# Windowed attention with global keys, then a softmax-gated feed-forward layer: queries and keys in runs of six tokens, token order, sums of the first batch by TensorE, a new order

## The chip, the cores and the metric

The kernel runs on one core of a Trainium2 chip. The metric is device time in microseconds (us), lower is better. A core has TensorE (PE in the profile, its weight loads PEld), VectorE (DVE), ScalarE (ACT), GpSimd (POOL) and SyncE (SP); SP, ACT and POOL can issue DMA transfers, which share 16 DMA engines. Each engine works through its own instructions in program order.

## What is computed

Inputs are q, k and v for 4 batches, 8 heads, 768 tokens and 64 dimensions. Every token attends to the last 96 tokens and to the first 8 (the global ones), with a bias that falls with distance by a slope per head. The result, 3072 tokens of 512 features, goes through a layer of width 1024 that is gated by its own softmax and normalised.

```python
is_global = pos[None, :] < int(n_global)
is_local = (rel >= 0) & (rel < int(n_local))
keep = is_global | is_local
dist = np.where(is_global & ~is_local, float(n_local), np.abs(rel).astype(np.float32))
bias = -slopes[:, None, None] * dist[None, :, :]
scores = np.where(keep, scores + bias[None, :, :, :], -1000000000.0)
a = np.exp(scores - np.max(scores, axis=-1, keepdims=True))
a = a / (np.sum(a, axis=-1, keepdims=True) + 1e-09)
x = a @ v                                  # then as [3072, 512]
h = x @ w_in
e = np.exp(h - h_max)
solu = h * e / (np.sum(e, axis=-1, keepdims=True) + 1e-09)
ln = (solu - mu) / np.sqrt(var + 1e-06) * g_ln
out = ln @ w_out
```

## The kernel before

**An order made ahead of time.** The kernel function first describes its work as steps: an engine, an estimated duration, a priority, the steps it needs and the buffers it takes and gives back. `Plan.order` is a list scheduler: it plays the steps through in time by their estimates, at each moment starting on each free engine the ready step of the lowest priority number whose buffers are free, and the sequence that comes out is the program order of every engine, SP's DMA queue included. The priorities are the list `PRIO`, one number per step. On the chip an engine stops at the first instruction whose input isn't there, whatever the plan thought, and what stands behind it waits too. DMAs have a pool of 8 in flight.

**Attention.** Two heads make a pair, 4 pairs (`p`) per batch (`b`). Queries and keys are loaded in runs of 8 tokens on a partition (`load_heads`, L498; 96 partitions for 768 tokens), cast to f16 on POOL (L698), transposed on PE (L714, eight transposes of 96 columns), and copied out of PSUM on DVE: keys in token order (`kT`, L733, a strided copy), queries in the order [place in the run, run] (`qT`, L729, a copy in order). So everything that follows query columns is in that order too and is read through views such as `p (j g) -> p j g`: the bias window `bw`, the exponentials `eb`, the sums and the products. Only the last product (L1019) writes `xT` in token order. The first 256 tokens of batch 0 come by a different load (`load_first`, L504), token by token.

For each group of key blocks of 64 and each pair, PE adds the bias (L822) and the scores (L840), 64x64 matmuls on the four quarters of the array, and ACT takes the exponential to `eb` (L848). Batch 0 has three groups of 256 queries, the others two of 384. For each unit of queries (`ui`; the same widths):

- `gs`: scores of the global keys for all heads at once (L883), exponential to `eg` (L894);
- `sm`: sums of all heads on PE with matrices of ones (L905 local, L912 global), one row per head, then ln (L920) and exp(-x) (L923) on ACT, the reciprocals `rr`;
- the reciprocals go to DRAM (`store_recip`, L553) and come back with each head's row on 64 partitions (`spread_recip`, L559, two loads), the tile `rb`;
- `av` and `aw`: the products with the values (L992) and with the global values `vgz` (L979), in two halves for two pairs at a time, each pair in a PSUM bank of its own; a one-element copy on DVE (`tick`, L1002) lies between the halves. The global product is a matmul of 64 rows by 128 columns for each half;
- `nm_`: DVE multiplies each bank by `rb` into `xT` (L1019).

The values of a batch are loaded in pieces (`load_v`, L511) and cast (L783); the first and last 64 tokens of each odd head come for all four batches in two loads (`load_ends`, L518) and are cast per batch (L797).

**Feed-forward.** For each tile of 128 tokens: G1 on PE (L1051, eight matmuls of 512 columns), exp on ACT (L1058), the gate on DVE (L1061), the sum of squares on ACT (L1065), eight transposes on PE (L1072) and their copy to `uT` (L1076, four buffers), G2 (L1110), and the scaled eviction (L1116) and store (L1118). Before the first G2, `w_out` is scaled by `g` on DVE (L625, eight instructions), its mean is taken on PE (L631) and subtracted on DVE (L635).

Of the kernel before, what the change touches and what calls it, by code (L numbers as in the profile page):

```python
# [18 lines left out]
P = 128  # L19
BLK = 64  # L20
WIN = 160
JW = 8
BG = BLK // JW
WG = WIN // JW
# [89 lines left out]
"""  # L114


class Plan:
# [129 lines left out]
def kernel(  # L247
# [119 lines left out]
    def v3(ap):  # L367
        return ap.rearrange("p (j g) -> p j g", j=JW)
# [794 lines left out]
```

## Time and profile before

| | us |
|---|---|
| median of 3 runs | 222.46 |
| range | 219.66 to 223.21 |
| profiled execution, its time | 223.18 |
| profiled execution, its span | 221.5 |

| engine | busy us | share of the span |
|---|---|---|
| ScalarE | 112.9 | 51% |
| VectorE | 112.6 | 51% |
| GpSimd | 65.0 | 29% |

The span runs from the first to the last instruction that the profile holds. The page cuts it into 40 slices of 5.5 us; a digit is the busy share in tenths, and for the clock the share of TensorE's full speed that was granted. A timeline row has the start, the duration, the engine, the line, what is written and read, and the count of merged instructions; in brackets stands the idle time of the engine ahead of it and what ended it. A group's row has busy us and the mean duration in ns behind the bar, then idle time ahead of the group by what ended it.

### The profile page before, as it was taken

How to read it: one execution, taken by the hardware profiler on the slowest of the kernel's cores; microseconds unless marked ns; L12 is line 12 of the kernel's file. 1: busy time of each engine (PE TensorE's matmuls, PEld its weight loads, DVE VectorE, ACT ScalarE, POOL GpSimd, SP SyncE). 2: the span in 40 equal slices, each digit the busy share in tenths (PEclk: the TensorE clock that was granted, in tenths of full speed). 3: DMA queues.
4: the chain of work that ended last, by engine and by line, in shares of the span. 5: the costliest groups of instructions: out<-in, count | busy, mean ns of one | idle time of the engine just before them, and what ended most of it. 6: DMA issues, size and time to landing. Idle time of an engine off the chain costs nothing. (4 is left out here: it accounts for less than half of the span.)

```text
span 221.5 us, 6271 instructions
## 1 busy us (share of the span) xinstructions
PE 174.9 (79%) x2636; PEld 103.2 (47%) x2636; DVE 112.6 (51%) x238; ACT 112.9 (51%) x202; POOL 65.0 (29%) x140
## 2 busy tenths in 40 slices
PE   0036837677988979997879989779997999998890
PEld 0014416555664646564544546455555455434440
DVE  0465367223574554865534656352772368484540
ACT  2003302432682367693455888364785674566752
POOL 7854187430392166433072008300100000000000
PEclk9999995555999999999988999999999999999998
DMA  6999999994299992999995039631603156300222
GB/s 178 252 202 304 189 206 206 235 259 91 66 259 253 291 222 69 238 251 269 248 231 132 18 113 225 146 145 50 145 0 147 22 130 143 142 3 0 95 95 96
DMA packets 47387, 35.23 MB, mean 159 GB/s; under 512 B 32440, under 2 KB 37120, under 8 KB 47360
## 3 DMA queue, kind: packets, MB, share of 16 engines
q1 hardware_dynamic: 44560, 33.24, 61.1%
q0 software_dynamic: 544, 1.05, 2.9%
q10 hardware_dynamic: 2256, 0.56, 1.1%
q8 instruction: 20, 0.33, 0.7%
q14 instruction: 7, 0.06, 0.1%
HBM read 29.50 MB, written 6.39 MB: 162 GB/s over the span
## 5 line engine op out<-in xcount | busy, mean ns | idle before, releaser
L848 ACT ACTIVATE eb<-bank 128x960 f16<-128x960 f32 (+3 forms) x36 | 29.9, 856 | 48.2 <-PE bank L840 47.7
L1051 PE MATMUL bank<-w_in_sb,xT 128*128 128x512 f16 x192 | 47.1, 389 | 0.1
L1110 PE MATMUL bank<-gw_out_sb,uT 128*128 128x512 f16 x192 | 44.8, 379 | 1.0 <-DVE xT L1019 0.4
L1061 DVE SCALAR_TENSOR_TENSOR uu<-ef,bank 128x1024 f16<-128x1024 f16 x24 | 29.2, 1216 | 12.5 <-ACT ef L1058 12.4
L1058 ACT ACTIVATE ef<-bank 128x1024 f16<-128x1024 f32 x24 | 24.5, 1020 | 16.3 <-PE bank L1051 16.2
L1019 DVE TENSOR_TENSOR xT<-bank,rb 128x384 f16<-128x384 f32 (+1 forms) x36 | 25.2, 730 | 10.1 <-PE bank L992 5.0
L1110 PEld LDWEIGHTS <-uT 128*128 128x128 f16 x192 | 17.8, 97 | 21.3 <-DVE uT L1076 1.4
L1051 PEld LDWEIGHTS <-xT 128*128 128x128 f16 x192 | 17.9, 99 | 20.3 <-issue 1.9
L1065 ACT ACTIVATE sq<-uu 128x1024 f16<-128x1024 f16 x24 | 25.2, 1051 | 3.9 <-DVE uu L1061 3.7
L714 PE MATMUL bank<-ident,k 96*128 96x96 f16 (+2 forms) x136 | 10.2, 220 | 19.5 <-POOL k L694 10.9
L733 DVE COPY kT<-bank 128x768 f16<-128x768 f16 (+2 forms) x20 | 15.4, 769 | 19.4 <-PE bank L714 16.8
L992 PE MATMUL bank<-eb,v 64*64 64x160 f16 (+4 forms) x464 | 20.5, 230 | 4.1 <-DVE tick L1002 1.3
L1076 DVE COPY uT<-bank 128x1024 f16<-128x1024 f16 x24 | 16.4, 689 | 14.1 <-PE bank L1072 6.1
L698 POOL CAST k<-k 96x1024 f16<-96x1024 f32 (+1 forms) x16 | 16.5, 1035 | 23.1 <-PE bank L714 11.3
L698 POOL CAST q<-q 96x1024 f16<-96x1024 f32 (+1 forms) x16 | 16.4, 1036 | 19.9 <-PE bank L714 13.3
L1116 ACT ACTIVATE osb<-bank,rstd 128x512 f32<-128x512 f32 x24 | 15.9, 684 | 11.2 <-PE bank L1110 5.3
L714 PEld LDWEIGHTS <-k 96*128 96x128 f16 (+2 forms) x136 | 7.9, 106 | 23.6 <-POOL k L694 11.1
L992 PEld LDWEIGHTS <-v 64*64 64x64 f16 x464 | 11.8, 107 | 12.1 <-issue 8.1
L822 PE MATMUL bank<-bw,identb 64*64 64x160 f16 (+4 forms) x448 | 16.0, 251 | 0.8 <-DVE uu L1061 0.6
L783 POOL CAST v<-v 128x704 f16<-128x704 f32 (+2 forms) x24 | 13.4, 576 | 10.7 <-DMA v<-in_v_dram 10.0
L840 PE MATMUL bank<-qT,kT 64*64 64x160 f16 (+4 forms) x416 | 15.6, 250 | 0.5 <-DVE qT L729 0.5
L1072 PE MATMUL bank<-ident,uu 128*128 128x128 f16 x192 | 14.4, 219 | 1.8 <-DVE uT L1076 0.9
(82 smaller groups left out, 176.3 us busy)
## 6 DMA issues: line engine op xcount, KB each, us to landing
out_dram<-osb SPq DMA_DIRECT2D x24, 256.0 KB
q<-in_q_dram SPq DMA_DIRECT2D x12, 384.0 KB
k<-in_k_dram SPq DMA_DIRECT2D x12, 384.0 KB
rb<-rd SPq DMA_DIRECT2D x12, 384.0 KB
v<-in_v_dram SPq DMA_DIRECT2D x12, 192.0 KB
w_out<-in_moe_w_out_dram SPq DMA_DIRECT2D x4, 512.0 KB
v<-in_v_dram SPq DMA_DIRECT2D x12, 160.0 KB
rb<-rd SPq DMA_DIRECT2D x6, 256.0 KB
```

Source lines behind the costliest of these rows:

```text
L698: nc.gpsimd.tensor_copy(out=o[0:w], in_=a[0:w].rearrange("p h j d -> p j h d"))
L714: nc.tensor.transpose(out=pt[:, j * m : j * m + m], in_=src[0:m, j].rearrange("p h d -> p (h d)"), identity=ident[0:m, 0:m])
L822: nc.tensor.matmul(out=sc[o : o + 64, par, col : col + n * JW], lhsT=identb[r, r], rhs=v3(bw[r, p])[:, :, a : a + n], start=(par, h) not i ...
L848: ex["fn"] = (lambda ex=ex, qk=qk, gw=gw: nc.scalar.activation(out=eb[at(qk, "eb")][:, :, 0:gw], in_=big(qk)[:, :, 0:gw], func=AF.Exp, sca ...
L992: nc.tensor.matmul(out=o_[64 * h : 64 * h + 64, :, gl : gl + m], lhsT=vv[r, v_at(vi, h, c), d0 + d, :], rhs=view(eb[at(e_own[b, gi, d0 + d ...
L1019: nc.vector.tensor_tensor(out=xT[at(xt_own[b], "xT")][:, p, q0:q1].rearrange("p (g j) -> p g j", j=JW), in0=one(av, d)[:, 0:w].rearrange(" ...
L1051: nc.tensor.matmul(out=ph()[:, ts(fh, 512)], lhsT=xT[at(xt_own[b], "xT")][:, j, ts(t % NA, P)], rhs=w_in_sb[:, j, ts(fh, 512)], start=(j = ...
L1058: ex["fn"] = lambda g1=g1, t=t, ph=ph: nc.scalar.activation(out=ef[at(g1, "ef")], in_=ph(), func=AF.Exp, accum_out=s0[:, t : t + 1])
L1061: u["fn"] = lambda u=u, g1=g1, t=t, ph=ph: nc.vector.scalar_tensor_tensor(out=uu[at(u, "uu")], in0=ef[at(g1, "ef")], scalar=USC, in1=ph(), ...
L1065: sqs["fn"] = lambda u=u, t=t: nc.scalar.activation(out=sq, in_=uu[at(u, "uu")], func=AF.Square, accum_out=s2[:, t : t + 1])
L1076: el["fn"] = lambda lt=lt, el=el: nc.vector.tensor_copy(out=uT[at(el, "uT")].rearrange("p c f -> p (c f)"), in_=one(lt).bitcast(FP16))
L1110: nc.tensor.matmul(out=one(g2), lhsT=uT[at(el_x, "uT")][:, c, :], rhs=gw_out_sb[:, c, :], start=(c == 0), stop=(c == NFC - 1))
```

## The change

The parts of the change:

1. **Runs of six on 128 partitions.** Queries and keys are loaded in runs of 6 tokens (4 in the second part of batch 0), cast with 768 (512) instead of 1024 elements a partition, and transposed in 6 (4) pieces of 128 columns.
2. **Token order.** Queries are copied out of PSUM in token order like the keys. `bw`, `gmask`, `eb`, the sums and products are in token order, so the views with `j` and `g` go.
3. **Sums of batch 0 by TensorE** (`DIRECT`). In its three units there is no `sm`, no store and no spread. `av` and `aw` handle one pair at a time: one bank takes the products with the values, the other the same matmuls with a block of ones (`onesv`, `onesz`, two constants that POOL makes), so that each sum stands on all 64 partitions of its head. ACT takes ln and exp of that bank per pair, and DVE multiplies by it.
4. **Global products in quarters.** For each half the 64x128 matmul becomes two of 64x64 on different quarters of the array, in all batches.
5. `w_out` is scaled by `g` on ACT instead of DVE.
6. The loads of the end blocks are split by batch (eight instead of two); `uT` has seven buffers instead of four.
7. **A new order.** Estimates are changed, the plan may hold at most four bulk loads in flight (`ldq`, an estimate's limit, no wait on the chip), and all priorities are new.

```diff
-JW = 8
-BG = BLK // JW
-WG = WIN // JW
+RUN = 6
...
+LDQ = 4
...
-    uT = many(4, [P, NFC, P], FP16, "uT")
+    uT = many(7, [P, NFC, P], FP16, "uT")
...
+    def constants_direct():
+        nc.gpsimd.memset(onesv, 1.0)
+        nc.gpsimd.tensor_copy(
+            out=onesz, in_=bass.AP(tensor=pick.tensor, offset=pick.offset,
+                                   ap=[pick.ap[0], pick.ap[1], [0, D]]))
...
+    DIRECT = {(0, 0), (0, 1), (0, 2)}
...
     def view(ebt, rows, par, col, n, lo, m):
-        return ebt[rows, par, col : col + n * JW].rearrange("p (j g) -> p j g", j=JW)[
-            :, :, lo : lo + m]
+        return ebt[rows, par, col : col + n][:, lo : lo + m]
...
-    def load_heads(src, dst, b, p, lo, hi):
+    def load_heads(src, dst, b, p, lo, run):
         rows = src[b, 2 * p]
-        n = hi - lo
         nc.sync.dma_start(
-            out=dst[0:n].rearrange("g h j d -> g h (j d)"),
-            in_=bass.AP(tensor=rows.tensor, offset=rows.offset + lo * JW * D,
-                        ap=[[JW * D, n], [S * D, 2], [1, JW * D]]))
+            out=dst[:, 0 : 2 * run * D].rearrange("g (h x) -> g h x", h=2),
+            in_=bass.AP(tensor=rows.tensor, offset=rows.offset + lo * D,
+                        ap=[[run * D, P], [S * D, 2], [1, run * D]]))
...
-            wr.append(step("DVE", 484, 16000 + 100 * j, [w_out_st[j // 2], g_st] + bias_st + [far_st], lambda j=j:
-                           nc.vector.tensor_scalar(
-                               out=gw_out_sb[:, j, :], in0=w_out32[:, j, :],
-                               scalar1=g32[:, j : j + 1], scalar2=None, op0=ALU.mult)))
+            wr.append(step("ACT", 640, 16000 + 100 * j,
+                           [w_out_st[j // 2], g_st] + bias_st + [far_st], lambda j=j:
+                           nc.scalar.activation(
+                               out=gw_out_sb[:, j, :], in_=w_out32[:, j, :], func=AF.Copy,
+                               scale=g32[:, j : j + 1])))
...
+                    if natural:
+                        nc.vector.tensor_copy(out=d_, in_=pt)
+                    else:
+                        nc.vector.tensor_copy(
+                            out=d_.rearrange("p (g j) -> p g j", j=run),
+                            in_=pt.rearrange("p (j g) -> p g j", j=run))
...
+            direct = (b, ui) in DIRECT
+            sm, bi, bd = None, None, []
+            if not direct:
+                sm = step("PE", (cols + w) * 0.42 + 60, tS, deps + [ge, sums_st, sumg_st], None,
+                          take=("one", "lns"), mode="s")
...
+            for ti_, duo in enumerate([(p, None) for p in range(NPR)] if direct else
+                                      [(p, p + 1) for p in range(0, NPR, 2)]):
...
+                        pv = duo[d]
+                        pair = duo[0] if pv is None else pv
+                        o_ = one(av, d)[:, 0:w]
+                        for h in range(2):
+                            x = h ^ par
+                            r = slice(64 * x, 64 * x + 64)
+                            if i < 0:
+                                nc.tensor.matmul(
+                                    out=o_[64 * h : 64 * h + 64, x * n : x * n + n],
+                                    lhsT=(onesz[r, 2 * pair + h] if pv is None else
+                                          vgz[r, b, 2 * pair + h, :]),
+                                    rhs=eg[at(gs, "eg")][r, 0:hw_],
+                                    start=False, stop=False,
+                                    tile_position=(64 * x, 64 * h), skip_group_check=True)
+                                continue
...
+                                lhsT=onesv[r, :] if pv is None else vv[r, v_at(vi, h, c), pair, :],
...
+                if direct:
+                    ln = step("ACT", 110 + w, ta + 1000, [aw, table_st], None, take="lns",
+                              free=[(av, 1)])
...
+                    re = step("ACT", 140 + w, ta + 1500, [ln], None, take="rr",
+                              free=[(ln, "lns")])
...
+                    nm_ = step("DVE", 40 + 1.34 * w, ta + 600 + 100 * d,
+                               [aw] + ([re] if direct else bd), None,
...
+                        r_ = rr[at(re, "rr")][:, 0:w] if direct else rb[at(bi, "rb")][:, p, 0:w]
+                        nc.vector.tensor_tensor(
+                            out=xT[at(xt_own[b], "xT")][:, p, q0:q1], in0=one(av, d)[:, 0:w],
+                            in1=r_, op=ALU.mult)
```

More of the change, by code (lines that the diff above doesn't have):

```diff
@@ L666, in do_part @@
         def do_part(i, lo, hi, p):
[L667 to L669 removed]
+            natural = b == 0 and i == 0
+            run = (hi - lo) // P
+            n = hi - lo
             for nm, src, x32, x16, dst, dn in (("k", k, k32, k16, kT, "kT"),
@@ L677, in do_part @@
                             nc.sync if nm == "k" else nc.scalar, src, nat[nm], a, 2 * p, 4),
-                            512 * 22 / 16, -80000 + 100 * p, [],
-                            eng="SP" if nm == "k" else "ACT")[1] for a in range(2)]
+                            512 * 20 / 16, -80000 + 100 * p, [],
+                            eng="SP" if nm == "k" else "ACT")[1] for a in range(run)]
                     need = nat_dma[nm]
                 else:
-                    iss, dma = load(lambda s, src=src, x32=x32, nm=nm, p=p, lo=lo, hi=hi, b=b:
-                                    load_heads(src, x32[at(s, nm + "32_")], b, p, lo, hi),
-                                    2 * w * 110 / 16, t0 - 6000, [],
-                                    take=(nm + "32_",))
+                    iss, dma = load(lambda s, src=src, x32=x32, nm=nm, p=p, lo=lo, run=run, b=b:
+                                    load_heads(src, x32[at(s, nm + "32_")], b, p, lo, run),
+                                    256 * (12 + 10.5 * run) / 16, t0 - 6000, [],
+                                    take=(nm + "32_",), bulk=True)
@@ L759, in do_v @@
                     P * (hi - lo) * 21 / 16, t0 - 6000, [first] if first else [],
-                    take=() if first else ("v32_",))
+                    take=() if first else ("v32_",), bulk=True)
                 first = first or iss
@@ L918 @@
-            sm["fn"] = sums
-            ln = step("ACT", 110 + w, tS + 1000, [sm], None, free=[(sm, "one")])
-            ln["fn"] = lambda sm=sm, w=w: nc.scalar.activation(
-                out=lns[at(sm, "lns")][:, 0:w], in_=one(sm)[:, 0:w], func=AF.Ln)
-            re = step("ACT", 140 + w, tS + 1500, [ln], None, take="rr", free=[(sm, "lns")])
-            re["fn"] = lambda re=re, sm=sm, w=w: nc.scalar.activation(
-                out=rr[at(re, "rr")][:, 0:w], in_=lns[at(sm, "lns")][:, 0:w], func=AF.Exp, scale=-1.0)
@@ new lines, with sums @@
+            sm, bi, bd = None, None, []
+            if not direct:
+                sm = step("PE", (cols + w) * 0.42 + 60, tS, deps + [ge, sums_st, sumg_st], None,
+                          take=("one", "lns"), mode="s")
+                def sums(sm=sm, gs=gs, todo=todo, w=w, hw_=hw_, b=b):
+                    sp = one(sm)[:, 0:w]
+                    ng_ = hw_
+                    for i, (gi, c, par, col, n, lo, gl, m) in enumerate(todo):
+                        for p in range(NPR):
+                            nc.tensor.matmul(
+                                out=sp[32 * p : 32 * p + 32, gl : gl + m], lhsT=onesd[:, par, :],
+                                rhs=view(eb[at(e_own[b, gi, p], "eb")], slice(0, P), par, col, n, lo, m),
+                                start=(i == 0), stop=False,
+                                tile_position=(0, 32 * p), skip_group_check=True)
+                    for x in range(2):
+                        for p in range(NPR):
+                            nc.tensor.matmul(
+                                out=sp[32 * p : 32 * p + 32, x * ng_ : x * ng_ + ng_],
+                                lhsT=onesg[:, x, p, :],
+                                rhs=eg[at(gs, "eg")][:, 0:hw_],
+                                start=False, stop=(x == 1),
+                                tile_position=(0, 32 * p), skip_group_check=True)
+                sm["fn"] = sums
+                ln = step("ACT", 110 + w, tS + 1000, [sm], None, free=[(sm, "one")])
+                ln["fn"] = lambda sm=sm, w=w: nc.scalar.activation(
+                    out=lns[at(sm, "lns")][:, 0:w], in_=one(sm)[:, 0:w], func=AF.Ln)
+                re = step("ACT", 140 + w, tS + 1500, [ln], None, take="rr", free=[(sm, "lns")])
+                re["fn"] = lambda re=re, sm=sm, w=w: nc.scalar.activation(
+                    out=rr[at(re, "rr")][:, 0:w], in_=lns[at(sm, "lns")][:, 0:w], func=AF.Exp, scale=-1.0)
+                di, dd = load(lambda s, re=re, w=w: store_recip(rd[at(s, "rd")], rr[at(re, "rr")], w),
+                              60, tS + 2000, [re], take=("rd",), iss=600)
+                plan.release(re, "rr", [dd])
+                bi = None
+                for h in range(2):
+                    own_b = bi
+                    s_, d_ = load(lambda s, di=di, h=h, w=w, own_b=own_b: spread_recip(
+                        rb[at(own_b or s, "rb")], rd[at(di, "rd")], h, w),
+                        256 * (12 + 0.28 * w / 1.0) / 16, tS + 4000, [dd] + ([bi] if bi else []),
+                        take=() if bi else ("rb",), iss=600)
+                    bi = bi or s_
+                    bd.append(d_)
+                plan.release(di, "rd", bd)
@@ new lines @@
+            lastu = ui == len(UNITS[b]) - 1
+            if lastu:
+                plan.release(kg_own[b], "kg", kg_users)
+                for p in range(NPR):
+                    plan.release(own[p, "k"], "kT", qk_of[p])
+                    plan.release(own[p, "q"], "qT", qk_of[p])
+            turn_of = []
+            by = [[x for x in todo if x[2] == par] for par in range(2)]
+            turns = [[(i, d) for i in range(max(map(len, by))) for d in (0, 1)
+                      if i < len(by[ph ^ d])] for ph in range(2)]
```

320 lines of the change are left out of this document (127 added, 193 removed), and 170 rows, old and new, of the table PRIO.

## The prediction

> **What bounds the kernel now.** I read the page first (engines, slices), then the busy time by stage, then the timeline of batch 0's first unit from its last exponential to its first feed-forward matmul, then the groups by shape for prices.
>
> ```profile
> PE 174.9 (79%) x2636; PEld 103.2 (47%) x2636; DVE 112.6 (51%) x238; ACT 112.9 (51%) x202; POOL 65.0 (29%) x140
> ...
> PEclk9999995555999999999988999999999999999998
> DMA  6999999994299992999995039631603156300222
> ```
>
> TensorE (PE) has the most work, but the slices show two regimes: up to slice 9 (50 us) the DMA engines are full and PE's clock falls to half; after it the clock is whole. The same by stage (columns: length, then busy us and instructions of PE, PEld, DVE, ACT, POOL, clock, DMA share, GB/s):
>
> ```profile
> 9.90:35.00 25.10, 13.86 (x177) 8.11 (x178) 13.77 (x39) 3.66 (x7) 13.35 (x23) 0.95 1.11 223
> 35.00:56.70 21.70, 16.27 (x402) 12.30 (x402) 8.83 (x17) 8.35 (x14) 7.25 (x9) 0.51 0.87 185
> 56.70:100.00 43.30, 39.05 (x657) 24.45 (x649) 25.98 (x54) 27.59 (x51) 20.43 (x34) 1.00 0.89 213
> 100.00:150.00 50.00, 42.71 (x714) 25.41 (x713) 26.61 (x51) 29.06 (x50) 15.40 (x18) 0.97 0.67 167
> 150.00:216.20 66.20, 63.01 (x700) 32.96 (x697) 35.58 (x73) 41.69 (x80) 0.73 (x4) 1.00 0.28 81
> 216.20:221.50 5.30, 0.00 (x0) 0.00 (x0) 0.00 (x0) 1.24 (x2) 0.00 (x0) 0.89 0.26 100
> ```
>
> From 56.7 to 216.2 us PE is busy 39.05+42.71+63.01 = 144.8 of 159.5 us; 14.7 us are idle. So the end is: start of the dense stage, plus 144.8 of work, plus 14.7, plus a tail of 5.3 (last eviction and store). What sets the start?
>
> ```profile
> 23.58 0.65 ACT L848 ACTIVATE eb<-bank 128x576 f16<-128x576 f32 x1 [0.27 <-PE bank L840]
> 25.56 0.42 ACT L923 ACTIVATE rr<-lns 128x256 f32<-128x256 f32 x1
> 27.60 0.62 SPq L553 DMA_DIRECT2D rd<-rr  x1
> 34.16 1.64 SPq L559 DMA_DIRECT2D rb<-rd  x2
> 37.83 0.39 POOL L783 CAST v<-v 128x256 f16<-128x256 f32 x1
> 39.82 0.74 POOL L797 CAST v<-vt 128x256 f16<-128x256 f32 x2 [0.61 <-DMA vt<-in_v_dram]
> 46.53 0.35 PE L992 MATMUL bank<-eb,v 64*64 64x160 f16 x4 [0.33 <-DVE kT L733]
> 51.59 0.59 DVE L1019 TENSOR_TENSOR xT<-bank,rb 128x256 f16<-128x256 f32 x1 [0.85 <-PE bank L992]
> 56.73 1.90 PE L1051 MATMUL bank<-w_in_sb,xT 128*128 128x512 f16 x8
> ```
>
> The reciprocals of unit 0 exist at 25.98 us. They go to DRAM (issued at 27.60), come back spread over partitions (issued at 34.16, behind bulk loads on SP's queue), and the first product that uses them runs at 51.59, 25.6 us later. The values' casts (pair 3 at 37.83, the end blocks at 39.82) are late too, but nothing hurried them. Units 1 and 2 fare no better: stores at 56.06, first product 73.42.
>
> ```profile
> 56.06 2.35 SPq L553 DMA_DIRECT2D rd<-rr  x2
> 73.42 0.59 DVE L1019 TENSOR_TENSOR xT<-bank,rb 128x256 f16<-128x256 f32 x1
> 25.58 3.57 PE L631 MATMUL bank<-gw_out_sb,onesm 128*128 128x512 f16 x8 [0.47 <-ACT lns L920]
> ```
>
> The clock counts besides: eight 512-column matmuls take 3.57 us at 25.58 and 1.90 at 56.73, so PE ran at half speed there too, whatever the 0.95 of that stage says.
>
> **The change part by part.**
>
> *Sums of batch 0 by TensorE.* The DRAM path goes for three units: 3 stores and 6 spreads of 256 KB (1.57 MB, 7 us of the queue at 223 GB/s; on SP 9 issues of about 0.6 us). In its place each pair's second bank gets the sums, already spread, and ACT takes ln and exp per pair. The first G1 can now come as early as: last exponential 24.23, four pairs of av/aw at half clock (46.53 to 51.59 held two such duos with their waits; about 1.2 us a pair), ln and exp 0.42 each (by L923), product 0.59: 30.5. The late end: values' pair 3 cast at 38.22, one more pair and the same 1.4: 40.9. Values and end blocks of this unit are 0.6 MB, 3 us at 223 GB/s; the change splits the end blocks by batch (two loads of 256 KB become eight of 64 KB, six more issues on SP, against the nine removed) and orders the loads anew, so I stay near the early end: **32 us instead of 56.7**.
>
> *What fills the 24.7 us.* Work that was there before stays: 16.27 us from 35 on at clock 0.51, 8.3 at full clock, and 0.8 from 32 to 35 by the mean of its stage (13.86 of 25.10, at half). PE idled 21.70-16.27 = 5.4 us in that stage waiting for keys and evictions; units 1 and 2 and batch 1 still come by the same queue, so I keep 5.4. Until the clock rises some time goes at half speed; the one dip of the dense stage (0.71 over 115 to 120 below) is 2.9 us at half, so 1.5 lost.
>
> ```profile
> 101.53 0.26 PE L979 MATMUL bank<-eg,vgz 64*128 64x192 f16 x2
> 101.72 0.38 PE L992 MATMUL bank<-eb,v 64*64 64x160 f16 x12
> 102.03 0.26 PE L979 MATMUL bank<-eg,vgz 64*128 64x192 f16 x2
> ...
> 102.35 0.39 PE L822 MATMUL bank<-bw,identb 64*64 64x160 f16 x12
> 102.56 0.39 PE L840 MATMUL bank<-qT,kT 64*64 64x160 f16 x12
> 102.79 0.33 PE L992 MATMUL bank<-eb,v 64*64 64x160 f16 x4
> ...
> 115.00:120.00 5.00, 5.00 (x27) 2.06 (x29) 1.55 (x2) 1.61 (x3) 2.77 (x3) 0.71 0.86 222
> 120.00:125.00 5.00, 5.00 (x66) 2.95 (x66) 3.26 (x7) 4.92 (x10) 0.00 (x0) 1.00 0.00 0
> ```
>
> *Global products in quarters.* Two 64x128 matmuls advance PE by 0.19 us (101.53 to 101.72): one after the other. Twelve 64x64 ones of 160 columns advance it by 0.31, four at a time in 0.10. Four quarters then cost 0.10 instead of 0.19; 24 halves in batches 1 to 3: -2.1. In batch 0 twice the halves at half the price: 0.
>
> *Doubled av in batch 0.* 128 more 64x64 matmuls at 0.31/12 = 26 ns, 88 sums matmuls fewer at the same rate: +1.0.
>
> *Token order.* Bias reads a contiguous row, scores a strided one, and they advance by 0.21 and 0.23 for twelve (102.35 to 102.56 to 102.79): a strided moving operand costs next to nothing. av also writes strided, 0.31 for twelve. If that is the reason, 336 matmuls in batches 1 to 3 save 28 x 0.09 = 2.5; else 0: half, -1.3. Transposes: 8x96 = 6x128 columns, 0.
>
> ```profile
> L1019 DVE TENSOR_TENSOR xT<-bank,rb 128x384 f16<-128x384 f32 x24 | 18.3, 797 | 6.8 <-PE bank L992 3.6 <-PE bank L912 1.5 <-PE bank L1110 1.0
> L635 DVE SCALAR_TENSOR_TENSOR gw_out_sb<-w_out,g,bank 128x512 f16<-128x512 f32 x8 | 5.9, 743 | 6.4 <-PE bank L631 5.0 <-PE bank L714 1.4
> L733 DVE COPY kT<-bank 128x768 f16<-128x768 f16 x12 | 11.5, 955 | 16.2 <-PE bank L714 13.7 <-ACT osb L1116 2.6
> L729 DVE COPY qT<-bank 128x768 f16<-128x768 f16 x12 | 6.6, 554 | 5.5 <-PE bank L714 2.8 <-PE bank L1110 1.5 <-PE bank L992 0.8
> L625 DVE TENSOR_SCALAR gw_out_sb<-w_out,g 128x512 f16<-128x512 f32 x8 | 3.6, 497 | 0.0
> L1116 ACT ACTIVATE osb<-bank,rstd 128x512 f32<-128x512 f32 x24 | 15.9, 684 | 11.2 <-PE bank L1110 5.3 <-PE bank L992 2.8 <-PE bank L1072 0.8
> PE bank L883 <- DVE xT L1019: 1.6, 3, 0.9
> PE bank L905 <- DVE xT L1019: 1.2, 1, 1.2
> PE bank L992 <- DVE xT L1019: 0.9, 2, 0.7
> ```
>
> *DVE.* The product now reads and writes in order: by L635's 743 ns for 512 contiguous elements, 384 take 557 instead of 797, -5.8 us over 24 (0 if order isn't the reason). Query evictions become strided like those of keys: 12 x (955-554) = +4.8. The eight weight scalings leave: -4.0. DVE stays near half busy; what counts is that PE waited 3.7 us for products after 56.7, of which 30% go: -1.1.
>
> *ACT.* Eight scalings at about 684 ns (+5.5) and nine more ln/exp pairs at 0.84 (+7.6). ACT was busy 12.0 of 46.8 us before the dense stage; that gap covers it. Without the cover it is the slower rival below. Each product of batch 0 now waits on DVE for its own ln and exp, and evictions for PE stand behind it: 0 if the next pair's av runs meanwhile, up to 12 x 0.84 = 10 if nothing does; four pairs in a row cover each other, 0. *POOL* casts 768 instead of 1024 elements: less work on an engine 29% busy, 0. *Loads* of queries and keys become 256 packets of 1.5 KB, the form of the 384 KB spreads:
>
> ```profile
> 92.70:99.20 6.50, 6.50 (x108) 4.35 (x107) 5.11 (x15) 5.18 (x12) 2.96 (x7) 1.00 1.04 255
> 108.30:115.20 6.90, 4.75 (x134) 3.37 (x131) 3.29 (x5) 4.38 (x7) 3.26 (x5) 0.95 1.05 224
> ```
>
> The first stage carried mostly spreads, the second mostly queries and keys: no loss, 0. *The new order and three more uT buffers*: no row prices them; ends -7 and +7 (half of the 14.7 us idle either way), taken as 0.
>
> **Sum.** Start 32; work 144.8 + 8.3 + 0.8 - 2.1 + 1.0 - 1.3 = 151.5; idle 14.7 - 1.1 = 13.6; new early losses 5.4 + 1.5 = 6.9; tail 5.3. Span 32 + 151.5 + 13.6 + 6.9 + 5.3 = 209.3 against 221.5, that is -12.2. The profiled run took 223.18 (1.7 outside its span), 0.7 over the median of 222.46; from the median: 210.3, say **210**.
>
> **Rivals.**
>
> *The clock stays at half until 56.7* (no change). For it: in 35 to 56.7 PE was 75% busy and had 0.51 all the same. Against it: dense G1 matmuls come now. Then 32 to 56.7 does (24.7-5.4)/2 = 9.7 us of the 151.5; the rest, 141.8 + 13.6 + 5.3, follows 56.7: span 217.4, from the median 218. The Trainium skill, page "TensorE: Matmul & The Clock Gate", Part 1 (the HAM clock gate), says that the clock falls to half after an idle window of about 3.4 us and rises after a busy one. By that rule early bursts between waits for loads would run cold, which is this rival; the trace agrees only in part, since the stage at 0.51 was 75% busy.
>
> *The loads set the pace.* DMA is full until 118 and nothing is loaded at 120 to 125; 101.5 us follow 120 in any case. The loads end earlier only by the 7 us of removed spreads: 215. Against it: PE was fully busy from 115 to 125, so loads weren't what it lacked then.
>
> *Slower: ACT waits for w_out.* The scalings wait for w_out's loads, and every exponential behind them on ACT's in-order queue waits too, and PE for those. Before, DVE held that wait. If w_out (2 MB) is loaded behind both batches' 9.4 MB and the 1 MB of w_in, it lands at about 58 at 223 GB/s; with 5.5 us of scalings G1 starts at about 66. With some 2 us saved elsewhere the time is 222.5 - 2 + (66 - 56.7) = 230. It decides from G1 later than 58.7, w_out later than about 51. Against it: G2 needs w_out soon after G1, so there is little reason to load it that late.
>
> **How the numbers follow.** A measurement of this kernel tells about 2% (218.0 to 226.9) from no change. Forecast (199 to 216) 0.60; loads set the pace 0.16; clock at half 0.13, two thirds of it within 2%; slower 0.11, a third of it within 2%. Faster 0.78, same 0.14, slower 0.08. The low end takes 30.5, none of the 6.9, the other half of token order (-1.2), and a small part of the order's -7: 199. The high end takes in the half clock and a part of the order's +7: 220; some 0.08 lie below and 0.12 above.
>
> **What would show it.** First G1 near 32 us, with batch 0's first product just before it; the granted clock at full from about 36; two quarters' groups in 0.10 us; the product of 384 near 560 ns and query copies near 955; PE idle after the first G1 near 20 us. Wrong would be: a first G1 after 45, half clock up to 55, ACT standing at the weight scaling, or PE idle grown beyond 27 us.

## The result and the profile after

The changed kernel takes 204.16 us (median of four runs, 202.19 to 204.68) against 221.98 us (219.66 to 223.21) for the kernel before beside it: ratio 0.921, 95% interval 0.911 to 0.932. The forecast was 210 us with a range of 199 to 220 and faster at 0.78. So direction and range were right, and the forecast lies 6 us too high. The profiled execution took 202.19 us, the fastest of the four, with a span of 200.5 us. Medians here and below count every execution, ratios only those within 1.5% of the fastest of their kernel, of which the kernel with whole global products has a single one (213.61 us), so that it gets no ratio.

The page of the changed kernel, the lines that answer to those shown of before:

```profile
PE 161.1 (80%) x2716; PEld 98.7 (49%) x2716; DVE 108.3 (54%) x236; ACT 123.1 (61%) x228; POOL 57.3 (29%) x142
...
PEclk9999996969999999999699999999999999999999
DMA  5999776995998996799459971011912662010223
```

PE was busy for 174.9 of 221.5 us before; now it is busy for 161.1 of 200.5. The span lost 21.0 us: 13.8 of busy time, though there are 80 more matmuls, and 7.2 of time in which PE is not busy. The clock is at half in three short dips, not in one long stretch. (The profile's record of the clock begins with a change, at 20.3 us here and at 29.2 in the kernel before, and the page shows 1.00 ahead of it. PE ran at half there in both: here transposes of 128 columns start 107 ns apart ahead of 20.3 us and 56 ns apart later, and in the kernel before the eight matmuls at 25.58 took 3.57 us instead of 1.90.) The stages (length, busy us and instructions of PE, PEld, DVE, ACT, POOL, clock, DMA share, GB/s):

```profile
11.10:31.86 20.76, 14.25 (x381) 10.90 (x380) 8.89 (x23) 9.45 (x19) 14.22 (x34) 0.97 0.88 198
31.86:57.00 25.14, 19.82 (x390) 12.82 (x389) 15.60 (x36) 18.37 (x40) 10.80 (x21) 0.89 0.87 270
57.00:100.00 43.00, 36.98 (x801) 25.25 (x799) 25.62 (x46) 27.63 (x46) 14.54 (x23) 0.96 0.88 235
100.00:150.00 50.00, 47.68 (x729) 27.22 (x722) 29.34 (x61) 36.13 (x67) 8.74 (x14) 1.00 0.49 123
150.00:195.30 45.30, 41.66 (x424) 22.30 (x424) 23.10 (x52) 29.01 (x56) 0.00 (x0) 1.00 0.27 81
195.30:200.50 5.20, 0.76 (x4) 0.14 (x2) 0.00 (x0) 1.27 (x2) 0.00 (x0) 1.00 0.34 128
```

The same sum as in the prediction: start 31.86; work 19.82 + 36.98 + 47.68 + 41.66 + 0.76 = 146.9; idle 17.3 in the four stages between; a tail of 5.20 - 0.76 = 4.4. Together 200.5. Batch 0's first unit, from its last exponential to its first feed-forward matmul, in the timelines of ACT, DVE and PE:

```profile
24.07 0.71 ACT L850 ACTIVATE eb<-bank 128x640 f16<-128x640 f32 x1
25.34 0.39 ACT L1018 ACTIVATE lns<-bank 128x256 f32<-128x256 f32 x1 [0.57 <-PE bank L1003]
...
28.82 0.42 ACT L1022 ACTIVATE rr<-lns 128x256 f32<-128x256 f32 x1 [0.21 <-DVE xT L1041]
```

```profile
27.74 0.98 DVE L1041 TENSOR_TENSOR xT<-bank,rr 128x256 f16<-128x256 f32 x2
...
30.40 0.41 DVE L1041 TENSOR_TENSOR xT<-bank,rr 128x256 f16<-128x256 f32 x1
```

```profile
30.87 1.06 PE L885 MATMUL bank<-qT,kg 128*64 128x128 f16 x16 [0.37 <-DVE xT L1041]
31.86 4.62 PE L1074 MATMUL bank<-w_in_sb,xT 128*128 128x512 f16 x16
```

The first product runs at 27.74 instead of 51.59, the last of the unit's four at 30.40, and G1 starts at 31.86 instead of 56.73. Where the kernel before had 25.6 us between reciprocals and product, the whole step from the last exponential to G1 now takes 7.1.

### The profile page after: what moved, and what is told of

It reads as the page before. It is cut to its first block, busy times and chain, and to the rows that moved or that the text cites. A ratio compares the mean times of both kernels' runs of the same rounds, so it can differ in the third digit from the quotient of the medians.

```text
span 200.5 us, 6454 instructions
## 1 busy us (share of the span) xinstructions
PE 161.1 (80%) x2716; PEld 98.7 (49%) x2716; DVE 108.3 (54%) x236; ACT 123.1 (61%) x228; POOL 57.3 (29%) x142
## 4 chain that ended last, share of the span: by engine, by line
PE 61%; DVE 16%; ACT 8%; issue 7%; POOL 6%; ACTq 0%; DVEq 0%; POOLq 0%
PE bank L1133 20%; PE bank L1074 16%; PE bank L723 6%; PE bank L1003 5%; PE bank L1095 4%; DVE qT L735 4%; DVE kT L735 3%; PE bank L824 3%; DVE xT L1041 2%; PE bank L842 2%; DVE uu L1084 2%; ACT osb L1139 2%; DVE uT L1099 2%; ACT sq L1088 2%; PE bank L885 2%
## 5 line engine op out<-in xcount | busy, mean ns | idle before, releaser
L1074 PE MATMUL bank<-w_in_sb,xT 128*128 128x512 f16 x192 | 45.7, 385 | 0.3
L1084 DVE SCALAR_TENSOR_TENSOR uu<-ef,bank 128x1024 f16<-128x1024 f16 x24 | 29.2, 1217 | 12.4 <-ACT ef L1081 12.3
L1081 ACT ACTIVATE ef<-bank 128x1024 f16<-128x1024 f32 x24 | 24.5, 1022 | 13.3 <-PE bank L1074 13.2
L1139 ACT ACTIVATE osb<-bank,rstd 128x512 f32<-128x512 f32 x24 | 16.3, 686 | 17.2 <-PE bank L1133 9.7
L1099 DVE COPY uT<-bank 128x1024 f16<-128x1024 f16 x24 | 16.2, 686 | 13.7 <-PE bank L1095 11.0
L723 PE MATMUL bank<-ident,q 128*128 128x128 f16 x96 | 8.7, 229 | 16.8 <-POOL ident L374 11.2
L1003 PE MATMUL bank<-eb,v 64*64 64x160 f16 (+4 forms) x464 | 18.6, 229 | 3.5 <-DVE tick L1013 1.2
L735 DVE COPY qT<-bank 128x768 f16<-128x768 f16 (+1 forms) x16 | 14.2, 888 | 11.9 <-PE bank L723 6.7
L1041 DVE TENSOR_TENSOR xT<-bank,rb 128x384 f16<-128x384 f32 x24 | 12.3, 552 | 11.0 <-PE bank L1133 4.2
L1003 PEld LDWEIGHTS <-v 64*64 64x64 f16 x464 | 14.9, 115 | 6.3 <-issue 6.0
L710 POOL CAST q<-q 128x768 f16<-128x768 f32 (+1 forms) x16 | 12.4, 775 | 18.5 <-PE bank L723 13.9
L785 POOL CAST v<-v 128x704 f16<-128x704 f32 (+2 forms) x24 | 13.5, 580 | 13.3 <-DMA v<-in_v_dram 13.2
L735 DVE COPY kT<-bank 128x768 f16<-128x768 f16 (+1 forms) x16 | 14.1, 888 | 5.6 <-PE bank L723 4.6
L710 POOL CAST k<-k 128x768 f16<-128x768 f32 (+1 forms) x16 | 12.3, 776 | 15.9 <-PE bank L723 14.0
L723 PEld LDWEIGHTS <-q 128*128 128x128 f16 x96 | 6.9, 101 | 19.6 <-POOL q L710 11.3
```

Source lines behind the costliest of these rows:

```text
L710: nc.gpsimd.tensor_copy(out=o, in_=a)
L723: nc.tensor.transpose(out=pt[:, j * P : j * P + P], in_=src[:, j, :], identity=ident)
L735: nc.vector.tensor_copy(out=d_.rearrange("p (g j) -> p g j", j=run), in_=pt.rearrange("p (j g) -> p g j", j=run))
L1003: nc.tensor.matmul(out=o_[64 * h : 64 * h + 64, gl : gl + m], lhsT=onesv[r, :] if pv is None else vv[r, v_at(vi, h, c), pair, :], rhs=view ...
L1074: nc.tensor.matmul(out=ph()[:, ts(fh, 512)], lhsT=xT[at(xt_own[b], "xT")][:, j, ts(t % NA, P)], rhs=w_in_sb[:, j, ts(fh, 512)], start=(j = ...
L1081: ex["fn"] = lambda g1=g1, t=t, ph=ph: nc.scalar.activation(out=ef[at(g1, "ef")], in_=ph(), func=AF.Exp, accum_out=s0[:, t : t + 1])
```

## The experiments

Twelve kernels ran, in four groups, each with the kernel before on the same chip. "Ratio" is to that kernel before, with its 95% interval; "busy" and "not busy" are PE's times in the profile of each (221.5 us of span before: 174.9 and 46.6).

| kernel | us | ratio | PE busy | not busy |
|---|---|---|---|---|
| changed, again | 205.02 | 0.9345 (0.929 to 0.940) | 163.8 | 39.4 |
| changed, whole global products | 218.11 | none | 181.0 | 35.4 |
| changed, averages in strided runs | 206.40 | 0.9379 (0.933 to 0.942) | | |
| changed, product strided | 208.67 | 0.9485 (0.944 to 0.953) | 165.1 | 42.0 |
| changed, scalings on DVE | 209.79 | 0.9352 (0.927 to 0.944) | | |
| changed, four uT buffers | 204.84 | 0.9278 (0.922 to 0.934) | 163.7 | 40.2 |
| before, no trip in batch 0 | 216.80 | 0.9787 (0.973 to 0.985) | 172.2 | 42.7 |
| before, quarters | 217.06 | 0.9797 (0.973 to 0.986) | 165.9 | 47.8 |
| before, quarters and no trip | 215.29 | 0.9614 (0.955 to 0.968) | 164.0 | 46.4 |
| before, formula order | 247.78 | 1.1154 (1.103 to 1.128) | | |
| changed, formula order | 235.99 | 1.0682 (1.059 to 1.078) | | |
| changed, formula order, with the trip | 239.86 | 1.0881 (1.080 to 1.096) | | |

### The changed kernel again

> The changed kernel once more, to have its time beside the next three: 204 us, ratio 0.92.

It took 205.02 us; its profile has the first G1 at 34.0 and a span of 203.2. The start of G1 thus moves by about 2 us between runs of one kernel, and 0.9345 is what the other variants of the changed kernel are held against.

### Whole global products in the changed kernel

```diff
+                        if i < 0:
+                            r = slice(64 * par, 64 * par + 64)
+                            src = onesz if pv is None else vgz[:, b]
+                            nc.tensor.matmul(
+                                out=o_[:, par * n : par * n + n],
+                                lhsT=src[r, 2 * pair : 2 * pair + 2, :].rearrange("r h d -> r (h d)"),
...
+                            continue
```

> The changed kernel with the global products as one 64x128 matmul per half and bank again, same order. My term: +2.1 us of TensorE work in batches 1 to 3, and about +2 in batch 0, where there are now twice as many halves; the local av matmuls keep their price (18 to 19 ns each). Time 207 to 208.5. Rival (hidden): TensorE idles elsewhere and takes it up, 204 to 205. Second rival (neighbourhood): the whole matmul also slows the local ones beside it, from 19 towards the 31 ns each that they cost before, 4 us more: 211 or above.

218.11 us, 13 us over the changed kernel run again; the fastest execution, 213.61, is 8.6 us over it. So the second rival held (211 or above). The page's line of engines, of an execution of 218.11 us, shows it as work, 181.0 us instead of 163.8:

```profile
PE 181.0 (84%) x2620; PEld 106.1 (49%) x2620; DVE 108.6 (50%) x236; ACT 123.5 (57%) x228; POOL 57.3 (26%) x142
```

Where it comes from is in PE's timeline. First this kernel, then the changed one again, both averaging a unit of a later batch at full clock (start, duration, line, count of merged matmuls):

```profile
102.06 0.26 PE L1012 MATMUL bank<-eb,v 64*64 64x160 f16 x4
102.26 0.26 PE L993 MATMUL bank<-eg,vgz 64*128 64x192 f16 x2
102.45 0.34 PE L1012 MATMUL bank<-eb,v 64*64 64x160 f16 x12
102.72 0.26 PE L993 MATMUL bank<-eg,vgz 64*128 64x192 f16 x2
```

```profile
115.28 0.26 PE L1003 MATMUL bank<-eb,v 64*64 64x160 f16 x4
115.37 0.25 PE L994 MATMUL bank<-eg,vgz 64*64 64x192 f16 x4
115.45 0.41 PE L1003 MATMUL bank<-eb,v 64*64 64x160 f16 x12
115.66 0.28 PE L994 MATMUL bank<-eg,vgz 64*64 64x192 f16 x4
```

Read the starts, not the durations. Four local matmuls hold the next group off by 0.20 us ahead of a whole product and by 0.09 ahead of quarters; two whole products by 0.19, four quarters by 0.08; twelve local matmuls by 0.27 and 0.21. The two whole products themselves run side by side: in the trace they start 4 ns apart (at 102.261 and 102.265), as the local matmuls of a group do. What costs is the change between the two tile sizes, once ahead of a group of whole products and once behind it, each time some 0.11 us more than the step between tiles of one size. It isn't peculiar to these tiles: in the kernel before, at full clock, a 128x128 transpose of 128 columns is followed by the next transpose after 56 ns, and by a 64x64 matmul after 149. PE's tile size changes 170 times in this kernel and 74 times in the changed one; the 96 more lie around the 48 groups of whole products.

To sum this up, PE's busy time is split so that each matmul gets the part that it adds behind the end of all matmuls before it. The 592 local matmuls then take 21.8 us here and 13.8 in the changed kernel run again, the global ones 10.0 and 4.7. That is 13.2 of the 17.2 us. A part of it is the clock: this kernel has 0.76 over 32 to 57 us and 0.81 over 57 to 80, the other 0.86 and 1.00. Behind 113 us, where both have the whole clock, the same 224 local matmuls take 6.5 and 4.7 us and the global ones among them 3.0 and 1.3: 3.5 us for 32 changes of size, 0.11 us each.

### Quarters in the kernel before

```diff
-                            r = slice(64 * par, 64 * par + 64)
...
-                                tile_position=(64 * par, 0), skip_group_check=True)
+                            for h in range(2):
+                                x = h ^ par
+                                r = slice(64 * x, 64 * x + 64)
...
+                                    lhsT=vgz[r, b, 2 * (d0 + d) + h, :],
...
+                                    tile_position=(64 * x, 64 * h), skip_group_check=True)
```

> The kernel before, in its own order and columns, with only the global products in quarters. After the run with whole global products in the changed kernel, a half of av has 0.27 us less with quarters, half of it in the local matmuls beside them: 24 halves of batches 1 to 3 give -6.5, 12 of batch 0 about -2.5; local av from 31 to about 19 ns each. Time 212 to 214. By the prediction's term (-2.1): 220 to 221. If TensorE's gaps take it up: no change.

Ratio 0.9797. By time (217.06 us) the expectation of 212 to 214 was missed, by work it was met: PE's busy time falls by 9.0 us, the time by 4.4.

```profile
PE 165.9 (78%) x2708; PEld 100.3 (47%) x2708; DVE 112.9 (53%) x238; ACT 112.8 (53%) x202; POOL 65.2 (30%) x140
```

By the same split, its 464 local matmuls go from 16.2 to 12.0 us and the global products from 6.7 to 2.9: 8.1 us in all, from the same order and the same strided views as before. The tile size changes 80 times instead of 152 (transposes of 96 and of 128 rows counted as one size: the step between those takes 56 ns, like that between two of one size). 72 changes at the 0.11 us found above are 7.9 us, an estimate. Between the two profiles the span falls by 7.8 us and the time that isn't busy grows from 46.6 to 47.8, so 1.2 us of the saved work turn into waiting. The medians lie closer together, 4.4 us, since the profiles are of the fastest execution of this kernel (215.36 us) and of one of the slowest of the kernel before (223.18).

### Are the strides the reason?

In batches 1 to 3 the changed kernel's local averages read and write in eight strided runs again. The averages there mix rows that don't belong together.

```diff
-                                out=o_[64 * h : 64 * h + 64, gl : gl + m],
+                                out=(o_[64 * h : 64 * h + 64, gl : gl + m] if pv is None or b == 0 else
+                                     o_[64 * h : 64 * h + 64].rearrange("p (j g) -> p j g", j=8)[
+                                         :, :, gl // 8 : (gl + m) // 8]),
```

> The changed kernel with the local av matmuls of batches 1 to 3 reading and writing in eight strided runs, as before; quarters, sums and order stay. Their columns come out permuted, so the result is not the reference's. If the strided write is what they paid before (theory of the prediction, with its upper bound or more): 336 matmuls go from 19 to about 26 to 31 ns each, 2.5 to 4 us, time 206.5 to 208.5. If strides are free and the whole global product beside them was the cause: 19 ns and 204.

206.40 us, ratio 0.9379; the interval overlaps that of the changed kernel. By the same split a local matmul of batches 1 to 3 takes 22 ns, as in the changed kernel, against 33 ns in the kernel before (the expectations put these at 19 and 31). The strided write, which the prediction held for a possible reason, costs nothing that can be measured.

### The trip, taken away in the kernel before

Batch 0's three units multiply by a constant tile that is there from the start, instead of the spread reciprocals, whose stores and spreads go.

```diff
-            di, dd = load(lambda s, re=re, w=w: store_recip(rd[at(s, "rd")], rr[at(re, "rr")], w),
+            di, dd = load(lambda s, re=re, w=w, b=b: b and store_recip(rd[at(s, "rd")], rr[at(re, "rr")], w),
...
-                                     in1=rb[at(bi, "rb")][:, p, 0:w].rearrange(
+                                     in1=(rb[at(bi, "rb")][:, p, 0:w] if b else rconst[:, 0:w]).rearrange(
```

> The kernel before, in its own order, with batch 0's stores and spreads of reciprocals left out; its products multiply by a constant tile, so batch 0 is not normalised. Theory of the prediction (the DRAM trip sets the start of the dense stage): the first product moves from 51.6 to at most 48 and the first G1 from 56.7 to at most 52; if the trip alone was the wait everywhere, G1 near 45 and a time of 211 or less. Rival (the order made for the trip holds it): av of batch 0 stands behind batch 1's key transposes on TensorE, so the first G1 stays above 50 and the time gains only some 2 to 5 us: 216 to 219.

216.80 us, ratio 0.9787. The trip is gone, and the first product hardly moves: the rival held. Rows of this kernel's POOL, DVE and PE timelines:

```profile
41.33 0.74 POOL L799 CAST v<-vt 128x256 f16<-128x256 f32 x2 [0.56 <-DMA vt<-in_v_dram]
```

```profile
43.84 0.96 DVE L735 COPY kT<-bank 128x768 f16<-128x768 f16 x1 [2.94 <-PE bank L716]
...
49.73 0.59 DVE L1021 TENSOR_TENSOR xT<-bank,rconst 128x256 f16<-128x256 f32 x1 [0.85 <-PE bank L994]
```

```profile
44.85 0.26 PE L994 MATMUL bank<-eb,v 64*64 64x160 f16 x4 [0.62 <-DVE kT L735]
...
54.75 2.27 PE L1053 MATMUL bank<-w_in_sb,xT 128*128 128x512 f16 x8
```

The first product runs at 49.73 instead of 51.59, though its factor was never late. It waits for the averages, these start at 44.85, when DVE has copied batch 1's keys out of PSUM (43.84 + 0.96), and the last values of the unit are cast only at 41.33 to 42.07. In the changed kernel the corresponding casts lie 20 us earlier, by its POOL timeline:

```profile
21.31 0.40 POOL L799 CAST v<-vt 128x256 f16<-128x256 f32 x1 [0.62 <-DMA vt<-in_v_dram]
21.66 0.40 POOL L785 CAST v<-v 128x256 f16<-128x256 f32 x1
```

So in the old order the trip lay under late values and late averages. Its removal alone brings the first G1 forward by 2.0 us, from 56.73 to 54.75. The 24.9 us of the changed kernel came with earlier values and a new order besides, and no run here separates these two.

### Both in the kernel before

The edits of the last kernel and of "quarters" together.

> Both of the two before at once, in the order of before. If they are separate terms their gains add: about 209 to 212. If they draw on the same idle time of TensorE: no better than the better of the two.

Ratio 0.9614 (0.955 to 0.968); the product of the two single ratios is 0.959. The two add up, though not to the 209 to 212 us that were expected, since each alone gave less than expected. From the page:

```profile
PE 164.0 (78%) x2708; PEld 99.6 (47%) x2708; DVE 112.6 (54%) x238; ACT 112.8 (54%) x202; POOL 65.4 (31%) x141
```

Its busy time is that of the changed kernel run again (163.8), its time that isn't busy still that of before (46.4, against 39.4). By these totals, what the rest of the change adds is less waiting, 7 us. They don't take the clock into account, which was 0.948 over this span and 0.974 over that of the changed kernel.

### The product in strides again

DVE's product in the changed kernel reads both operands and writes in a permuted order, as before.

```diff
-                            out=xT[at(xt_own[b], "xT")][:, p, q0:q1], in0=one(av, d)[:, 0:w],
-                            in1=r_, op=ALU.mult)
+                            out=xT[at(xt_own[b], "xT")][:, p, q0:q1].rearrange("p (g j) -> p g j", j=8),
+                            in0=one(av, d)[:, 0:w].rearrange("p (j g) -> p g j", j=8),
+                            in1=r_.rearrange("p (j g) -> p g j", j=8), op=ALU.mult)
```

> The changed kernel with the DVE products reading their two operands in the old permuted way (columns come out permuted, not the reference's result), same order. Mean of the 384-wide product from 552 back to about 797 ns, DVE +8 us. By the prediction (products are on TensorE's waits only in part): +1 to +2 us, 205 to 206. Rival (DVE sets banks free late everywhere): +4 or more, 208. Rival (all hidden): 204.

208.67 us; against the changed kernel run again the ratios stand as 0.9485 to 0.9345, 1.5% or 3.1 us, with an error of 0.7% from the two intervals. That lies between the theory's 1 to 2 us and the rival's 4. The groups by shape, first of this kernel, then of the changed one:

```profile
L1041 DVE TENSOR_TENSOR xT<-bank,rb 128x384 f16<-128x384 f32 x24 | 18.2, 798 | 10.5 <-PE bank L1134 3.9 <-ACT osb L1140 2.8 <-PE bank L1003 2.0
```

```profile
L1041 DVE TENSOR_TENSOR xT<-bank,rb 128x384 f16<-128x384 f32 x24 | 12.3, 552 | 11.0 <-PE bank L1133 4.2 <-ACT osb L1139 3.0 <-ACT lns L925 1.8
```

798 ns against 552: the order of access sets the price. DVE gets 8.4 us more work (116.7 against 108.3) and is busy 56% of the span; still the time rises by 3. Of the rise in span (203.2 to 207.1) 1.3 us are PE busy and 2.6 are PE waiting. What PE waits for is in the trace. Its waits that a product of DVE ended, in this kernel (total us, times, longest):

```profile
PE bank L1003 <- DVE xT L1041: 1.1, 2, 0.7
PE bank L723 <- DVE xT L1041: 0.9, 2, 0.5
PE bank L1096 <- DVE xT L1041: 0.9, 1, 0.9
PE bank L824 <- DVE xT L1041: 0.6, 1, 0.6
PE bank L885 <- DVE xT L1041: 0.5, 1, 0.5
PE bank L1134 <- DVE xT L1041: 0.3, 1, 0.3
```

Together 4.3 us; in the changed kernel run again they are 1.5. The 2.8 us more account for PE's longer waiting.

### The scalings back on DVE, and four uT buffers

```diff
-                           nc.scalar.activation(
-                               out=gw_out_sb[:, j, :], in_=w_out32[:, j, :], func=AF.Copy,
-                               scale=g32[:, j : j + 1])))
+                           nc.vector.tensor_scalar(
+                               out=gw_out_sb[:, j, :], in0=w_out32[:, j, :],
+                               scalar1=g32[:, j : j + 1], scalar2=None, op0=ALU.mult)))
```

> The changed kernel, same order, with the eight scalings of w_out on DVE again. ACT does 5.5 us less and DVE 4.0 us more, both before 52 us. If ACT's scalings hold exponentials back (the slower rival's mechanism, in small): faster by 1 to 2 us, 203. If DVE is what batch 0 waits for: slower by 1 to 3, 206 to 208. The prediction took both as covered: 204 to 205.

Ratio 0.9352 against 0.9345: no difference by the ratios, to about 1%. More can't be said, since the raw times scatter from 206.22 to 211.65.

```diff
-    uT = many(7, [P, NFC, P], FP16, "uT")
+    uT = many(4, [P, NFC, P], FP16, "uT")
```

> The changed kernel with four buffers for the transposed hidden state instead of seven, same list of priorities. Theory, the prediction's value (the three more buffers are worth nothing by themselves): within 1 us of the changed kernel run again, 204 to 206 us, ratio near 0.93. Rival, the buffers are a part of the gain (transposed states wait for second matmuls to give buffers back, and PE with them): 207 to 212 us, with PE idle before the evictions of the transposed states.

204.84 us, ratio 0.9278: the three buffers are worth nothing by themselves.

### Both kernels without their lists of priorities

Where `PRIO` is empty the planner orders the steps by its own formula, from estimates that the change has altered too.

```diff
-PRIO = """
...
+PRIO = ""
```

> The kernel before without its list of priorities: the planner orders the steps by its own formula, the work is the same. Theory (the parts of the change give most of the gain in any order; the list gives the early first G1): only the measure for the next two, 220 to 235 us. Rival (the list alone carries before's time): over 240.

> The changed kernel without its list of priorities, ordered by the same formula as the run beside it. Theory, parts in any order (quarters with their neighbours and the clock 2 to 4.5 us, the product in order 3.7, fewer transposes, no trip): the ratio to the kernel before ordered by the formula is 0.92 to 0.95. Rival, the new order carries the gain: ratio over 0.97, and first G1 later than 45 us.

247.78 and 235.99 us. Without its list the old kernel takes 11.5% more, so here the rival held (over 240). Its first G1, at 44.6 us, comes 12 us earlier than with the list, and the kernel is slower all the same, so an early start alone doesn't make a short time. In the changed kernel the formula's first G1 comes at 36.8. Between the two, in formula order, the change is worth 1.0682 / 1.1154 = 0.958 (with an error of 0.013 from the two intervals), which lies between what the two theories gave. With the lists it is worth 0.9345. The rest, 2.4% with an error of about 1.5%, is what the new list does beyond the old one, if the parts are worth the same in both orders; changed estimates are in that number as well.

With `DIRECT = set()` besides, batch 0 makes the trip again:

> As the last, with batch 0's sums by spread, store and load again as in the other batches. Theory, the trip holds the first rows: first product 8 to 20 us later than in the last run, and the time longer by 3 to 10 us. Rival, the doubled average products and the nine more ln/exp pairs of batch 0 cost as much as the trip: within 2 us of the last run, or below it.

239.86 us, 1.9% over the last (error 1.2%), in the theory's range by time. But the first product moves by 6 us only, not 8 to 20. The product's rows, first of the direct kernel, then of this one (shortest, median and longest ns, first and last start):

```profile
L953 DVE TENSOR_TENSOR xT<-bank,rr x12: 414/415/425, 31.1 to 71.8; 128x256 f16<-128x256 f32 x12
```

```profile
L953 DVE TENSOR_TENSOR xT<-bank,rb x12: 412/415/424, 37.2 to 75.5; 128x256 f16<-128x256 f32 x12
```

The first G1 moves by 2.1 us, from 36.8 to 38.9. In this order, too, the trip was partly covered. Removing it is worth about 2% in either kernel (0.9787 in the kernel before, where nothing took its place; 1 / 1.019 here, where the doubled products and the nine ln/exp pairs did).

## Why the prediction was right, and where it was off

Term by term, against the 209.3 us of span that were forecast and the 200.5 of the profile:

| term | forecast | measured |
|---|---|---|
| first G1 | 32 | 31.9 (34.0 run again, 33.9 with four uT buffers) |
| work from there, with 1.5 lost to the clock | 153.0 | 146.9 |
| idle | 13.6 + 5.4 = 19.0 | 17.3 |
| tail | 5.3 | 4.4 |

**The start was right, its cause only half.** The prediction named the trip and gave the late values as its upper bound. The runs show that the trip by itself holds little: without it the old order starts G1 at 54.75. The number came out because the change moves the values as well, which the prediction supposed ("orders the loads anew") and didn't show; so far it was luck.

**The work was mis-sized, by 6.1 us.** The failed step is the pricing of quarters. The prediction took -2.1 us for the global products of batches 1 to 3, and the trace has 4.53 going to 2.47, -2.1. But it priced them alone. Their neighbours, the local averages of the same batches, went from 10.9 to 7.5 us, -3.4, where it had put -1.3 under "token order" with the strided write as reason. The size came from the quarters, as their removal and their addition showed, and the reason given was wrong, as the strided averages showed. That is 2.1 us of the 6.1. Both misreadings have one root: where it took two whole products to run "one after the other", and twelve local matmuls to pay for strides, the starts contain the changes of tile size. In batch 0, where it put nothing for quarters, local and global products together went from 7.5 to 4.9 us in the run that has the quarters alone, 2.6 more. Further 2.1 lie ahead of the start: PE is busy for 14.25 us between 11.1 and 31.86 now, and for 12.13 in the same stretch of before:

```profile
11.10:32.00 20.90, 12.13 (x159) 6.90 (x160) 10.99 (x33) 3.66 (x7) 9.83 (x20) 1.00 1.13 227
```

So the new order not only starts G1 early, it also does more ahead of it. Against this stands the clock: behind the first G1 PE is busy at half clock for 8.8 us, which loses 4.4 where the prediction put 1.5. Together that is some 4 of the 6.1 us; the rest isn't assigned. Behind the row of quarters stands a rule: the Trainium skill, page "TensorE: Matmul & The Clock Gate", Part 3, says that matmuls on different tiles of the array run side by side. The traces agree (twelve local ones in 0.21 us, 18 ns each), and show besides that tiles of another size among them cost 0.11 us at each change.

**The product was right in its duration and too small in its worth.** 552 ns against a forecast of 557. The prediction gave it 1.1 us of idle time, 30% of the 3.7 us that PE waited for products; its undoing costs 3.1 us, and PE's waits for products grow from 1.5 to 4.3. So the waits were the right place to look, and the 30% was too small: it is the cut in the product's duration (from 797 to 557 ns), while a wait that ends with a product can go altogether.

**DVE's and ACT's other terms.** Query copies came out as forecast (955 ns), and the scalings on ACT too (5.5 us). They were hidden: the run with scalings on DVE isn't slower or faster by its ratio, to about 1%.

```profile
L735 DVE COPY qT<-bank 128x768 f16<-128x768 f16 x12 | 11.5, 955 | 10.9 <-PE bank L723 5.9 <-PE bank L1133 3.1 <-PE bank L1095 1.2
```

```profile
L638 ACT ACTIVATE gw_out_sb<-w_out,g 128x512 f16<-128x512 f32 x8 | 5.5, 710 | 0.0
```

**uT and the new order at nothing.** Right for the buffers. Probably not for the order: about 2.4% of its own beside the old list, within the bounds of 7 us either way that stood there. Where it lies in the sum isn't shown; of the 19.0 us of idle time that were forecast it can have saved little, since 17.3 were measured. That 210 was too high comes from the pricing of the quarters and probably from this.

**The rivals.** *Clock at half until 56.7*: false. It is at half twice between 30 and 45 us, each time for less than 5 us. *The loads set the pace*: false, since PE is busy for 19.82 of the 25.14 us behind the first G1 while DMA is at 0.87, and the time is 11 us below the 215 of this rival. *ACT waits for w_out*: false; the scalings start at 32.49 and lie between exponentials with no idle time ahead of them (the group above: 0.0). The last two end at 51.44, and the means and the first G2 follow:

```profile
51.85 1.89 PE L644 MATMUL bank<-gw_out_sb,onesm 128*128 128x512 f16 x8
...
60.74 0.59 PE L1133 MATMUL bank<-gw_out_sb,uT 128*128 128x512 f16 x2
```

## What to carry to other kernels

Price a matmul together with its neighbours: where PE goes from tiles of one size to another it lost 0.11 us at each change here, so cutting the odd ones to the size of the rest can save more than they take themselves (here 8.1 us where the global products took 6.7). Before a long chain is cut, look for the next thing that is late behind it (here values and averages), for otherwise the cut gives little (here the first product came 1.9 us earlier, of a chain of 25.6). And work isn't time: part of what is saved or added goes into waiting, in either order (9.0 us less of busy time shortened the span by 7.8 in the old order, 17.2 us more lengthened it by 13.2 in the new one).

## What was unexpected of the hardware

**A change of tile size.** Some 0.11 us each, at full clock: around 64x128 products among 64x64 matmuls, and 149 instead of 56 ns behind a 128x128 transpose. A local matmul comes to 33 ns between whole products and 22 ns between quarters. Why the change costs this isn't shown.

**A busy PE doesn't always get its clock back.** Windows of 2 us in the kernel before, then in the changed one (PE busy is the first figure behind the length, the clock the third from the end):

```profile
36.00:38.00 2.00, 2.00 (x60) 1.71 (x60) 1.93 (x4) 0.67 (x2) 1.54 (x3) 0.50 1.28 197
38.00:40.00 2.00, 2.00 (x60) 1.63 (x61) 0.98 (x2) 1.33 (x3) 1.39 (x3) 0.50 1.08 232
40.00:42.00 2.00, 2.00 (x72) 1.80 (x64) 0.79 (x2) 1.55 (x3) 0.68 (x3) 0.50 1.13 195
```

```profile
38.00:40.00 2.00, 0.45 (x9) 0.45 (x9) 1.52 (x4) 1.68 (x4) 0.00 (x0) 1.00 1.05 386
40.00:42.00 2.00, 1.97 (x77) 1.75 (x78) 1.72 (x6) 1.52 (x5) 0.83 (x1) 0.68 1.07 398
42.00:44.00 2.00, 2.00 (x94) 2.00 (x88) 0.48 (x3) 1.63 (x5) 0.00 (x0) 0.50 1.07 401
44.00:46.00 2.00, 1.19 (x40) 0.87 (x33) 1.16 (x3) 1.95 (x6) 1.01 (x2) 0.96 0.46 155
```

The changed kernel loses its clock behind a sparse stretch (0.45 us busy of 2) and is at half from about 40.7 to 44.2 us, by these rows; after some 3.4 us of work it has its clock back. The rule of the Trainium skill, page "TensorE: Matmul & The Clock Gate", Part 1, is a busy window of about 3.4 us, and here the trace agrees. The kernel before was busy for 6 us without a gap in these rows and stayed at 0.50; there it doesn't. Where it lies in time can be a part of the reason. In these traces the clock keeps a state for 3.41 us or a multiple of it (23.89 in this stretch, from 32.58 us on), and of the steps of 3.41 us only one, from 35.99 to 39.40, lies wholly in the busy stretch from 35.97 to 42.16. In the kernel without the trip nearly the same matmuls fall otherwise against these steps, and the clock comes back at 41.88:

```profile
38.00:40.00 2.00, 1.97 (x52) 1.53 (x53) 0.87 (x2) 1.35 (x3) 1.65 (x3) 0.50 1.16 210
40.00:42.00 2.00, 2.00 (x76) 1.80 (x67) 0.90 (x2) 1.43 (x3) 1.44 (x3) 0.53 1.14 237
42.00:44.00 2.00, 0.59 (x26) 0.41 (x27) 0.16 (x1) 0.46 (x1) 0.99 (x2) 1.00 1.13 231
```

All these stretches are of small matmuls, and those of the kernel before and of the one without the trip hold transposes as well. What else the clock goes by isn't settled by these runs.

**Strides cost DVE and not PE.** Reading and writing in eight runs makes DVE's product 798 instead of 552 ns; on PE the same views leave a local matmul at 22 ns.
